# Retention and two MoE layers on one core: where moving and stationary operands begin within 64 bytes

## The chip, the cores and the metric

The kernel runs on one core of a Trainium2 chip. The metric is the device time of an execution, in microseconds, and the median over runs.

## The reference

Three layers follow each other. Batch 4, 8 heads, 768 positions, head size 64 give 3072 tokens of 512 features.

```python
# retention: per head a state S (64x64)
state = gamma * state + outer(k[t], v[t])
y[t]  = scale * q[t] @ state
# layer 1 (d_ff 2048)
h = x @ w_in
x = (h * sigmoid(1.702 * h)) @ w_out
# layer 2 (d_ff 1536)
gate = sigmoid(x @ w_gate)
out  = (gate * (x @ w_val)) @ w_out
```

Inputs are float32, the weights arrive as 64-bit words and are brought to float32 on the chip.

## The kernel before

**Products with three matmuls.** Nearly every product of 128x128 with 128x512 is done three times in float32r: each operand is split into a high part (a cast on ACT) and a low part (the original less the high part, on DVE or POOL), and high times high, high times low and low times high are summed in PSUM. In a matmul one operand is *stationary* (the weights that are loaded into the array, 128 columns) and one is *moving* (512 columns stream past it).

**Phase 1** goes through six blocks of 512 tokens. The attention of a block is worked out in items that are dealt out between the matmuls of the block before. For each block and each of 16 slices of d_ff there is a *unit*: `proj` (lines 268 to 273) multiplies the slice's weights `wh`, `wl` (stationary) with the block's tokens `xh`, `xl` (moving), twelve matmuls; `gated` and `gated_lo` make `gh`, `gl`; two units later `emit_out` (lines 357 to 382) multiplies the output weights `wh`, `wl` (stationary) with `gh`, `gl` (moving), twelve matmuls into four accumulators. The first eight units do this second product in plain float32, on unsplit tiles (line 373). `split_w` (lines 260 to 265) makes `wh` and `wl` in a pool of four. The tokens `xh`, `xl` lie in one of two pools, `xe` for even blocks and `xo` for odd ones (lines 59 and 299). The first two blocks are done half a d_ff at a time.

**Phase 2** has three groups of 1024 tokens and in each three rounds over a third of d_ff. A round has four *chains* (gate and value of two pairs of slices). A chain is seven products of 256-column halves that are combined so that eight are not needed: `product` (lines 526 to 536) multiplies chain weights `oh`, `ol` (stationary, made in `split_chain`, lines 515 to 524) with token halves and differences `xoh`, `xol` (moving), 42 matmuls in all. Chains alternate between two pools for their weights, `we` for even chains and `wo` for odd ones (`p2["w"][n % 2]`). `consume` (lines 543 to 563) makes the gated values `g2h`, `g2l`. At the end of a round `out_products` (lines 649 to 656) multiplies them with the output weights: here `g2h`, `g2l` are stationary and `woh`, `wol` move, 96 matmuls in a round.

**What sets the order.** It is written out by hand (`tc.manual_schedule`): each engine does its instructions in the order of the code. Pools are stacked from the left end and from the right end of a partition's memory (`left`, `right`, lines 49 to 65); a tile's place follows from the sizes of those before it.

**Where tiles begin.** The right-hand pools grow down from byte 229,344 of a partition, which is 32 past a multiple of 64, and nearly all tiles are multiples of 64 bytes long. So all that lies there up to the small constant tiles, and again behind them, begins 32 bytes past a multiple of 64; the left-hand pools begin at a multiple. The line that makes a weight pair in the kernel before:

```python
wh = wsp_p.tile([P, 512], F32R, name="wh", tag="wh")
```

Of the kernel before, what the change touches and what calls it, by code (L numbers as in the profile page):

```python
# [8 lines left out]
F32 = mybir.dt.float32  # L9
F32R = mybir.dt.float32r  # L10
# [5 lines left out]
P = 128  # L16
# [8 lines left out]
def retention_moe_moe2(  # L25
# [23 lines left out]
    left, right = (ctx.enter_context(ExitStack()) for _ in range(2))  # L49

    def pool(stack, name, bufs, side, **kw):
        return stack.enter_context(tc.tile_pool(name=name, bufs=bufs, side=side, reuse_waits="tile", **kw))

    PSUM = dict(space=bass.MemoryType.PSUM)
    dram = ctx.enter_context(tc.tile_pool(name="dram", bufs=1, space=bass.MemoryType.DRAM))
    wraw_p = pool(left, "wraw", NW, "left")
    wsp_p = pool(left, "wsp", 4, "left")
    g_p = pool(left, "g", 2, "left")
    x_p = [pool(right, "xe", 1, "right"), pool(left, "xo", 1, "left")]
    const = pool(right, "const", 1, "right")  # L60
# [15 lines left out]
    dv_sb = const.tile([P, CPB - 1, H], F32, name="dv_sb")  # L76
    dc_sb = const.tile([P, H], F32, name="dc_sb")
    dg_sb = const.tile([P, KC], F32, name="dg_sb")
    dm_sb = const.tile([P, 2, KC, C], F32, name="dm_sb")
    R = [const.tile([P, KC, P], F32, name=f"R{i}") for i in range(2)]  # L80

# [118 lines left out]
    def stage(n=1):  # L200

        for _ in range(min(n, len(to_stage))):
            ph, f, k = to_stage.popleft()
            t = cv_p.tile([P, 512], U64, name="w64", tag="w64", bufs=4)
            nc.sync.dma_start(out=t, in_=(w1 if ph == "1" else w2)[f, k])
            staged.append((ph, f, k, t))

    def convert(n, lo_engine):
# [48 lines left out]

        return scale, upper, lower, total

    def split_w(raw, lo_engine):  # L260
        wh = wsp_p.tile([P, 512], F32R, name="wh", tag="wh")
        wl = wsp_p.tile([P, 512], F32R, name="wl", tag="wl")
        nc.scalar.copy(wh, raw)  # L263
        lo_engine.tensor_tensor(out=wl, in0=raw, in1=wh, op=ALU.subtract)  # L264
        return wh, wl
# [74 lines left out]
    def split_out(i):  # L340

        j = i - DEPTH
        if WHOLE <= j < len(units):
            w_t[j, "out"] = split_w(raw1[units[j][1], 1], nc.gpsimd)

    def split_for(i):

        if i < len(units):
            b, f = units[i]
            w_t[i, 0] = split_w(raw1[f, 0], nc.gpsimd if i < 3 * FH else nc.vector)  # L350
# [65 lines left out]
    p2 = {}  # L416
# [14 lines left out]
    def tmp(name, bufs):  # L431
        return p2["tmp"].tile([P, 512], F32, name=name, tag=name, bufs=bufs)
# [82 lines left out]
    def split_chain(n, late):  # L515


        t, pl = wraw8[n], p2["w"][n % 2]
        a, b, engine = (S3, S4 + 1, nc.gpsimd) if late else (S1, A12 + 1, nc.vector)
        h, l = (pl.tile([P, b - a, 256], F32R, name=f"{x}{late:d}", tag=f"{x}{late:d}") for x in ("oh", "ol"))  # L520
        nc.scalar.copy(h, t[:, a:b])  # L521
        for j in range(a, b):
            wo[n, j] = (h[:, j - a], l[:, j - a])
        return lambda: engine.tensor_tensor(out=l, in0=t[:, a:b], in1=h, op=ALU.subtract)  # L524
# [13 lines left out]
    cb, gt, sgt, woh = {}, {}, {}, {}  # L538
# [4 lines left out]
    def consume(n, which, c):  # L543

        g, r, p, m = chains[n]
        if m == 0:
            yield
            sgt[p, which] = sg = tmp("sg", 4)
            nc.scalar.activation(out=sg, in_=c, func=AF.Sigmoid)
            yield  # L550
            yield
            return
        f, half = 2 * p + which // 2, which % 2
        if which == 0:
            for j in range(2):
                gt[f + j] = [p2["g2"].tile([P, 2, 512], F32R, name=x, tag=x) for x in ("g2h", "g2l")]
        gh, gl = (t[:, half, :] for t in gt[f])
        nc.vector.tensor_tensor(out=c, in0=c, in1=sgt.pop((p, which)), op=ALU.mult)
        yield
        nc.scalar.copy(gh, c)  # L560
        yield
        nc.vector.tensor_tensor(out=gl, in0=c, in1=gh, op=ALU.subtract)
        yield
# [12 lines left out]
    def middle(n):  # L576

        a, m1 = cb[n]
        b, d = bank2("pb"), bank2("pd")
        ahead = n + 1 < len(chains)  # L580
        if ahead and (n + 1) not in early:
            early[n + 1] = split_chain(n + 1, False)
        product(n, b, A12, B21, True, True)
        add(b, b, m1)
        while carried:
            next(carried.pop())
        c11 = consume(n, 0, b)
        next(c11)
        product(n, a, S2, T2, False, True)
        u2 = tmp("u2", 1)  # L590
        nc.scalar.copy(u2, a)
        if whole:
            whole.pop()
            split_out2()
        next(c11)
        if ahead:
            early.pop(n + 1)()
        product(n, d, S1, T1, True, True)
        product(n, a, S3, T3, False, True)
        u3, c22 = tmp("u3", 1), tmp("c22", 1)  # L600
        nc.scalar.copy(u3, a)
        next(c11)
        add(c22, d, u3)
        cb[n] = [a, d, u2, c22]

    def finish(n, last):
        a, d, u2, c22 = cb.pop(n)
        x22, x21, x12 = (consume(n, j, c) for j, c in ((3, c22), (2, a), (1, d)))
        next(x22)
        product(n, a, A22, T4, False, True)  # L610
        next(x22)
        next(x21)
        if not last:
            next(x22)
        product(n, d, S4, B22, False, True)
        next(x21)
        if last:
            next(x21)
        add(d, d, u2)
        next(x12)  # L620
        next(x22 if last else x21)
        if not last and n + 2 < len(chains):
            early[n + 2] = split_chain(n + 2, False)
        next(x12)
        if last:
            next(x12)
        else:
            carried.append(x12)
# [48 lines left out]
    with tc.manual_schedule():  # L677
# [9 lines left out]
        for t in range(1, 4):  # L687
            for i in (Q, K, V, KN):
                load_in(t, i, wraw_p, "wraw")
            stage()  # L690
        sig = const.tile([P, 1], F32, name="sig")
        nc.vector.memset(sig, 0.0)
        nc.scalar.activation(out=sig, in_=sig, func=AF.Sigmoid)
        warm = cv_p.tile([P, 512], F32, name="warm", tag="cva", bufs=3)
# [39 lines left out]
        for i, (b, f) in enumerate(units):  # L734
# [21 lines left out]
            n = blocks1[b][1]  # L756
# [30 lines left out]
            if b == len(blocks1) - 1:  # L787
                if f == 9:
                    sums(0)
                elif f in (11, 13):  # L790
                    split_chain(0, f == 13)()
# [144 lines left out]
```

## Time and profile before

| | |
|---|---|
| median of 3 runs | 1207.12 us (1205.52 to 1207.32) |
| span of the profiled execution, first to last instruction | 1204.5 us |
| the rest of a run's time, median less span | 2.6 us |
| PE busy | 1183.9 us (98%), 5916 matmuls |
| weight loads (PEld) | 948.8 us (79%) |
| DVE, ACT, POOL busy | 794.6, 541.4, 532.5 us |
| DMA queue q1 | 121.54 MB, 31.1% of 16 engines' span |
| HBM read, written | 98.31 MB, 24.12 MB |

The profiled execution's own time is listed as its span. Matmuls are pipelined, so a matmul's listed duration is longer than the distance to the start of the next; the ends are modelled, the starts are recorded. The plain float32 matmuls are recorded as two passes each, which is why PE has 5916 and not 5250. In the chain of waits a piece of PE is as long as the distance from one start (or end) to the next.

### The profile page before, as it was taken

How to read it: one execution, taken by the hardware profiler on the slowest of the kernel's cores; microseconds unless marked ns; L12 is line 12 of the kernel's file. 1: busy time of each engine (PE TensorE's matmuls, PEld its weight loads, DVE VectorE, ACT ScalarE, POOL GpSimd, SP SyncE). 2: the span in 40 equal slices, each digit the busy share in tenths (PEclk: the TensorE clock that was granted, in tenths of full speed). 3: DMA queues.
4: the chain of work that ended last, by engine and by line, in shares of the span. 5: the costliest groups of instructions: out<-in, count | busy, mean ns of one | idle time of the engine just before them, and what ended most of it. 6: DMA issues, size and time to landing. Idle time of an engine off the chain costs nothing.

```text
span 1204.5 us, 16042 instructions
## 1 busy us (share of the span) xinstructions
PE 1183.9 (98%) x5916; PEld 948.8 (79%) x5916; DVE 794.6 (66%) x1050; ACT 541.4 (45%) x948; POOL 532.5 (44%) x398
## 2 busy tenths in 40 slices
PE   7899999999999999999999999999999999999998
PEld 6656878877788887788788888888888888888887
DVE  6989999687588677766664636368535458535454
ACT  5424444444444444444554626164626164626151
POOL 5557874222322332322454626257625257635340
PEclk9999999999999999999999999999999999999999
DMA  8644245534335333412202202043212133212111
GB/s 324 208 160 140 88 158 167 192 115 140 123 100 163 123 114 133 131 52 79 70 1 88 80 27 79 27 135 110 72 34 71 36 115 115 86 35 70 37 36 70
DMA packets 62575, 123.48 MB, mean 103 GB/s; under 512 B 6816, under 2 KB 16288, under 8 KB 62496
## 3 DMA queue, kind: packets, MB, share of 16 engines
q1 hardware_dynamic: 61920, 121.54, 31.1%
q8 instruction: 46, 0.75, 0.3%
q10 hardware_dynamic: 576, 0.92, 0.2%
q14 instruction: 33, 0.27, 0.1%
HBM read 98.31 MB, written 24.12 MB: 102 GB/s over the span
## 4 chain that ended last, share of the span: by engine, by line
PE 87%; DVE 7%; issue 2%; DMA 2%; POOL 2%; ACT 1%; ACTq 0%; SPq 0%; DVEq 0%; POOLq 0%
PE pa L532 17%; PE pd L532 8%; PE acc L377 6%; PE h L273 6%; PE h L272 6%; PE h L271 6%; PE acc L378 6%; PE acc L379 6%; PE pb L532 4%; PE po L655 4%; PE po L656 4%; PE po L654 4%; DVE cva L234 2%; PE h L142 2%; DVE cva L231 2%
## 5 line engine op out<-in xcount | busy, mean ns | idle before, releaser
L264 POOL TENSOR_TENSOR wl<-wraw,wh 128x512 fp32r<-128x512 f32 x112 | 163.4, 1465 | 298.1 <-ACT wh L263 297.6
L273 PE MATMUL h<-xh,wl 128*128 128x512 f32 x384 | 152.0, 396 | 3.1 <-POOL wl L264 2.9
L271 PE MATMUL h<-xh,wh 128*128 128x512 f32 x384 | 154.2, 402 | 0.8 <-ACT xh L187 0.7
L272 PE MATMUL h<-xl,wh 128*128 128x512 f32 x384 | 150.9, 393 | 0.2 <-DVE xl L188 0.2
L377 PE MATMUL acc<-gh,wh 128*128 128x512 f32 x352 | 142.2, 404 | 1.4 <-DVE half L396 1.4
L378 PE MATMUL acc<-gh,wl 128*128 128x512 f32 x352 | 137.9, 392 | 0.0
L379 PE MATMUL acc<-gl,wh 128*128 128x512 f32 x352 | 137.2, 390 | 0.0
L263 ACT CAST wh<-wraw 128x512 fp32r<-128x512 f32 x184 | 109.1, 617 | 35.4 <-PE acc L379 34.6
L524 POOL TENSOR_TENSOR ol<-raw,oh 128x768 fp32r<-128x768 f32 x36 | 67.0, 1862 | 127.2 <-ACT oh L521 127.2
L281 ACT ACTIVATE sg<-h 128x512 f32<-128x512 f32 x88 | 52.6, 598 | 146.4 <-PE h L273 146.3
L282 DVE TENSOR_TENSOR sg<-h,sg 128x512 f32<-128x512 f32 x88 | 60.6, 688 | 86.3 <-ACT sg L281 85.9
L532 PE MATMUL pa<-xol,oh 128*128 128x512 f32 x288 | 114.0, 396 | 0.0
L532 PE MATMUL pa<-xoh,oh 128*128 128x512 f32 x288 | 113.3, 393 | 0.0
L532 PE MATMUL pa<-xoh,ol 128*128 128x512 f32 x288 | 112.8, 392 | 0.0
L287 ACT CAST gh<-sg 128x512 fp32r<-128x512 f32 x88 | 54.6, 621 | 98.2 <-DVE sg L282 98.2
L644 POOL TENSOR_TENSOR wol<-wor,woh 128x512 fp32r<-128x512 f32 x36 | 57.1, 1586 | 87.8 <-ACT woh L643 87.8
L273 PEld LDWEIGHTS h<-xh,wl 128*128 128x128 f32 x384 | 72.1, 188 | 23.5 <-POOL wl L264 6.9
L271 PEld LDWEIGHTS h<-xh,wh 128*128 128x128 f32 x384 | 72.2, 188 | 18.7 <-issue 1.7
L272 PEld LDWEIGHTS h<-xl,wh 128*128 128x128 f32 x384 | 72.1, 188 | 18.0 <-issue 1.9
L234 DVE SCALAR_TENSOR_TENSOR cva<-w,cva 128x512 uint32<-128x512 uint32 x68 | 84.4, 1241 | 2.3
L655 PE MATMUL po<-wol,g2h 128*128 128x512 f32 x216 | 84.4, 391 | 0.0
L656 PE MATMUL po<-woh,g2l 128*128 128x512 f32 x216 | 84.2, 390 | 0.0
(132 smaller groups left out, 2598.5 us busy)
## 6 DMA issues: line engine op xcount, KB each, us to landing
w<-in_w_dram SPq DMA_DIRECT2D x68, 512.0 KB, 3.7
in_t<-in_qkv_dram SPq DMA_DIRECT2D x93, 256.0 KB, 3.6
raw<-w2d SPq DMA_DIRECT2D x72, 256.0 KB, 3.1
w2d<-cva SPq DMA_DIRECT2D x36, 256.0 KB, 2.2
wor<-w2d SPq DMA_DIRECT2D x36, 256.0 KB, 2.7
out_dram<-ost SPq DMA_DIRECT2D x23, 256.0 KB, 2.0
xt<-x2d SPq DMA_DIRECT2D x18, 256.0 KB, 4.3
x2d<-ost SPq DMA_DIRECT2D x14, 256.0 KB, 2.8
```

The source lines that it names most:

```text
L234: nc.vector.scalar_tensor_tensor(out=ai, in0=hi, scalar=0x80000000, in1=ai, op0=ALU.bitwise_and, op1=ALU.bitwise_or)
L263: nc.scalar.copy(wh, raw)
L264: lo_engine.tensor_tensor(out=wl, in0=raw, in1=wh, op=ALU.subtract)
L271: nc.tensor.matmul(bank[:, :n], wh[:, k, :], xh[:, k, :n], start=(k == 0), stop=False)
L272: nc.tensor.matmul(bank[:, :n], wh[:, k, :], xl[:, k, :n], start=False, stop=False)
L273: nc.tensor.matmul(bank[:, :n], wl[:, k, :], xh[:, k, :n], start=False, stop=(k == KC - 1))
L377: nc.tensor.matmul(a, wh[:, wc], gh[:, :n], start=st, stop=False)
L378: nc.tensor.matmul(a, wl[:, wc], gh[:, :n], start=False, stop=False)
L379: nc.tensor.matmul(a, wh[:, wc], gl[:, :n], start=False, stop=sp)
L532: nc.tensor.matmul(bank, w[:, kk], x[:, k, :], start=start and k == 0 and w is wh and x is xh, stop=stop and k == 1 and w is wl, skip_grou ...
L655: nc.tensor.matmul(bank, gh, wl, start=False, stop=False)
L656: nc.tensor.matmul(bank, gl, wh, start=False, stop=f == FR - 1)
```

## The change

Tiles are moved within 64 bytes. A tile of 32 bytes, `edge`, is put at the right end ahead of all others, and the small tile `sig` is made among the constants instead of behind them; with both, all right-hand tiles that matmuls stream from begin at a multiple of 64 bytes. A function `shifted` makes a tile 16 elements (64 bytes) longer than needed and uses it from a given element on; the stationary operands of the three-matmul products are made with it.

| operand of the products | before: bytes past a multiple of 64 | after |
|---|---|---|
| `xh`, `xl` of even blocks (moving) | 32 | 0 |
| `xh`, `xl` of odd blocks (moving) | 0 | 0 |
| `wh`, `wl` of phase 1, both products (stationary) | 0 | 16 |
| `gh`, `gl` (moving) | 0 | 0 |
| `xoh`, `xol` (moving) | 32 | 0 |
| `oh`, `ol` of even chains (stationary) | 32 | 48 |
| `oh`, `ol` of odd chains (stationary) | 0 | 8 |
| `g2h`, `g2l` (stationary) | 0 | 40 |
| `woh`, `wol` (moving) | 0 | 0 |

The operands of attention's float32 matmuls go from 32 (some from 0) to 0.

```diff
+    pool(ctx, "edge", 1, "right").tile([P, 8], F32, name="edge")
...
+    sig = const.tile([P, 1], F32, name="sig")
...
+    def shifted(pool_, name, shape, floats, **kw):
+        n = 1
+        for d in shape[1:]:
+            n *= d
+        t = pool_.tile([shape[0], n + 16], F32R, name=name, tag=name, **kw)[:, floats:floats + n]
+        return t if len(shape) == 2 else t.rearrange("p (a b) -> p a b", a=shape[1])
+
     def split_w(raw, lo_engine):
-        wh = wsp_p.tile([P, 512], F32R, name="wh", tag="wh")
-        wl = wsp_p.tile([P, 512], F32R, name="wl", tag="wl")
+        wh = shifted(wsp_p, "wh", (P, 512), 4)
+        wl = shifted(wsp_p, "wl", (P, 512), 4)
...
-        h, l = (pl.tile([P, b - a, 256], F32R, name=f"{x}{late:d}", tag=f"{x}{late:d}") for x in ("oh", "ol"))
+        h, l = (shifted(pl, f"{x}{late:d}", (P, b - a, 256), 2 if n % 2 else 12) for x in ("oh", "ol"))
...
-                gt[f + j] = [p2["g2"].tile([P, 2, 512], F32R, name=x, tag=x) for x in ("g2h", "g2l")]
+                gt[f + j] = [shifted(p2["g2"], x, (P, 2, 512), 10) for x in ("g2h", "g2l")]
...
-        sig = const.tile([P, 1], F32, name="sig")
```

## Rows read from the trace of the kernel before

**Rows 1.** The page, parts 1 and 2: busy time, share and count; granted clock in tenths.

```profile
PE 1183.9 (98%) x5916; PEld 948.8 (79%) x5916; DVE 794.6 (66%) x1050; ACT 541.4 (45%) x948; POOL 532.5 (44%) x398
...
PEclk9999999999999999999999999999999999999999
```

**Rows 2.** Busy time by stretch: PE, PEld, DVE, ACT, POOL (counts), granted clock, DMA, GB/s.

```profile
0.00:60.00 60.00, 49.01 (x432) 36.91 (x433) 47.78 (x71) 28.65 (x62) 32.38 (x29) 1.00 0.76 266
60.00:120.00 60.00, 56.17 (x242) 36.88 (x241) 53.82 (x68) 22.17 (x40) 37.97 (x27) 0.97 0.47 152
120.00:180.00 60.00, 58.44 (x251) 46.45 (x250) 59.32 (x64) 28.73 (x54) 47.65 (x31) 1.00 0.38 123
180.00:300.00 120.00, 120.00 (x746) 96.79 (x745) 92.33 (x135) 54.77 (x100) 40.78 (x30) 1.00 0.47 152
...
780.61:841.30 60.69, 60.69 (x265) 49.51 (x264) 43.61 (x52) 32.06 (x55) 38.62 (x27) 1.00 0.34 111
```

**Rows 3.** Groups by form on PE and PEld: count, busy us, mean ns, idle before.

```profile
L271 PE MATMUL h<-xh,wh 128*128 128x512 f32 x384 | 154.2, 402 | 0.8 <-ACT xh L187 0.7
...
L377 PE MATMUL acc<-gh,wh 128*128 128x512 f32 x352 | 142.2, 404 | 1.4 <-DVE half L396 1.4
...
L271 PEld LDWEIGHTS h<-xh,wh 128*128 128x128 f32 x384 | 72.2, 188 | 18.7 <-issue 1.7 <-ACT xh L187 0.9 <-ACT wh L263 0.5
```

**Rows 4.** PE's timeline in an odd block (block 3): start us, us, instruction.

```profile
415.39 0.40 PE L378 MATMUL acc<-gh,wl 128*128 128x512 f32 x1
...
417.90 0.39 PE L271 MATMUL h<-xh,wh 128*128 128x512 f32 x1
...
420.39 0.39 PE L273 MATMUL h<-xh,wl 128*128 128x512 f32 x1
```

**Rows 5.** The same in an even block (block 4).

```profile
467.26 0.40 PE L271 MATMUL h<-xh,wh 128*128 128x512 f32 x1
...
468.20 0.40 PE L272 MATMUL h<-xl,wh 128*128 128x512 f32 x1
468.44 0.40 PE L273 MATMUL h<-xh,wl 128*128 128x512 f32 x1
...
469.84 0.40 PE L273 MATMUL h<-xh,wl 128*128 128x512 f32 x1
```

**Rows 6.** Chain of waits, pieces of an odd chain, then an even one: start, us.

```profile
734.01 1.40 PE pd L532 x6
...
736.79 1.37 PE pa L532 x6
738.16 1.36 PE pd L532 x6
```

**Rows 7.** PE's timeline, output products of a round: the first and the sixty-first start.

```profile
761.55 0.39 PE L654 MATMUL pd<-woh,g2h 128*128 128x512 f32 x1
...
775.15 0.40 PE L532 MATMUL pa<-xoh,oh 128*128 128x512 f32 x1
```

**Rows 8.** Chain of waits: eight passes of plain float32 in phase 1.

```profile
98.76 3.43 PE acc L373 x8
```

**Rows 9.** ACT's timeline, casts for successive chains; the page's group of POOL's subtractions.

```profile
725.16 1.05 ACT L521 CAST oh<-raw 128x1024 fp32r<-128x1024 f32 x1
...
735.26 1.05 ACT L521 CAST oh<-raw 128x1024 fp32r<-128x1024 f32 x1
...
L264 POOL TENSOR_TENSOR wl<-wraw,wh 128x512 fp32r<-128x512 f32 x112 | 163.4, 1465 | 298.1 <-ACT wh L263 297.6
```

**Rows 10.** PE's timeline in an even chain: two neighbouring starts.

```profile
651.60 0.39 PE L532 MATMUL pa<-xoh,oh 128*128 128x512 f32 x1
651.82 0.39 PE L532 MATMUL pa<-xol,oh 128*128 128x512 f32 x1
```

## The prediction, made before the changed kernel ran

> **What bounds the kernel now.** I read the page's first two parts first. [...] Then the busy time by stretch: after the first 180 us PE is busy for all of each stretch, and before that it is idle for 11.0, 3.8 and 1.6 us of three times 60 [rows 2]. So from 180 us on nothing is late for PE, and the time is the number of matmuls times the distance between two starts. A PE that is always "busy" can still be slow, so I read the distance from the starts in the timeline and from the pieces of the chain of waits, not from the durations: a matmul of 512 columns is listed with 0.39 us, but the next starts after 0.23.
>
> Nearly all work is one form, a float32r matmul of 128x512 whose weights are loaded while the one before streams (188 ns of weight load, one for each matmul) [rows 3]. By the loops there are 4584: 576 projections of even blocks, 576 of odd blocks, 1056 of phase 1's second product, and in phase 2 nine rounds of 168 chain and 96 output matmuls, 2376. Their start-to-start distance differs with nothing but the place of the operands:
>
> - moving and stationary operand both at a multiple of 64 bytes: an odd block's twelve projections stand 226 ns apart (2.49 us in 11 steps), and the output products of phase 2 stand 13.60 us / 60 = 226.7 ns apart [rows 4, 7]. Behind an interruption by attention some steps are longer: over the second product and the projection together it is 5.00 / 22 = 227.3 [rows 4].
> - both 32 bytes off (even chains): 2.73 / 12 = 227.5 ns [rows 6].
> - moving 32 off, weights at a multiple: an even block's projections stand 2.58 / 11 = 234.5 ns apart, with a single step of 0.24 among them [rows 5]; an odd chain takes 1.40 / 6 = 233.3 [rows 6].
>
> A round of phase 2, one part of each kind, is 60.69 us for 264 matmuls, 229.9 each [rows 2]. [...]
>
> **What the change does, part by part.** No instruction is added, removed or moved on any engine. One wait for a DMA, once in the kernel, where phase 2 opens, stands one instruction earlier on ACT, on a copy into `u2` or `u3` and not on the sigmoid behind it. I cost it at nothing: it is the same load, and ACT has time to wait, idle for over half of each stretch [rows 2]; at the most it is one such instruction's place in a queue that PE does not wait for in that stretch.
>
> *Moving operands to multiples of 64.* This touches the even blocks' projections (234.5 ns) and all chains. Alone, with weights that fit, the step would be the locked one, 226.7: it saves 576 x 7.8 = 4.5 us in phase 1 and 2376 x 3.2 = 7.6 in phase 2; the other 1632 of phase 1 lose their rest, 0.6 each, 1.0. Together 13.1 us.
>
> *Weights off by 16, 48, 8 and 40.* No row has such a place. All steps of the kernel, also the 1632 + 864 that are now at 226.7, get a new one, so this is the larger term and the unknown one. [...] What is known is that displacing the weights by half of 64 bytes moves the step by 233.3 - 226.7 = 6.6 ns, and that single steps of about 0.22 occur between longer ones [rows 10]. [...] I take half of the known effect, as a gain: 226.7 - 3.3 = 223.4 ns, near those short steps. Then phase 2 saves 2376 x (229.9 - 223.4) = 15.4 us, the 1632 save 1632 x 3.9 = 6.4, the even blocks 576 x 11.1 = 6.4, in all 28.2. This includes the 13.1 above.
>
> What of it lies on the path: from 180 us on all of it. In the first 180 us PE waits 16.4 us for others [rows 2], so a shorter step becomes a longer wait; I take off a tenth of the phase 1 part, 1 us. Does something else then come late? DVE is busy 92 of 120 us in the fullest stretch behind 180 us, and POOL 41 of 120 [rows 2]; 3% less time leaves both below 80%.
>
> *Writes into displaced tiles.* ACT and DVE or POOL write the halves. A cast into a chain's tile takes 1.05 us whether it lands 32 off or at a multiple [rows 9], so I cost it at nothing. Offsets of 8 and 16 have no row. A worse price is covered: POOL waits 297.6 us for ACT in the weight splits [rows 9]; were each of its subtractions (1465 ns, 112 of them) half as long again, 82 us, that wait would shrink first. Without that cover each microsecond would count, in the first 180 us above all. From below, a cheaper write gains nothing, as PE does not wait for it there.
>
> The sum is made on the profiled execution: span 1204.5 - 27.2 = 1177.3. The median of the three runs, 1207.12, is 2.6 us over that span, for what lies around it, so 1180 us.
>
> [...] The rows show the step of one and the same moving stream at 227.5 or 233.3 ns with weights in two places [rows 6]. [...]
>
> **The rivals.**
>
> 1. *Only the moving side counts; weights off are neither good nor bad.* Every step is 226.7: 13.1 us, with 1 us for the start 12, so 1195. For: 226.7 is what all well-placed rows settle on, sixty in a row [rows 7]. Against: weights do matter in the chains [rows 6].
> [...]
> 3. *Slower: what is good is that both operands stand alike.* The two fast kinds in the rows, 0 with 0 and 32 with 32, are alike, and the slow one is not [rows 4, 6]; after the change nothing is alike. The place is every stream of both phases, the price 233.3 a step: phase 2 loses 2376 x 3.4 = 8.1 us, the 1632 of phase 1 lose 9.8, the even blocks gain 0.7: +17.2, so 1224. It decides as soon as the mean step is over 229.6, what the 4584 have now (weighting 229.9, 227.3 and 234.5). For: it is the plainest reading of the four kinds of rows. Against: "alike" may only stand for one good displacement among several. At 240 for all it would be +48, 1255.
> [...]
>
> **How the numbers follow.** My forecast (1180, its own range 1172 to 1188) 0.32; rival 1 (1195) 0.20; rival 2 (1165) 0.20; rival 3 (1224, between 1210 and 1235) 0.19; rival 4 0.09. A measurement of this kernel can tell 0.2%, 2.4 us, from no change. Faster: 0.32 + 0.20 + 0.20 = 0.72; same, of rival 4 and the edge of 1 and 3, 0.08; slower 0.20. The range takes in rivals 1 and 2 but for the part below 1160 (0.06), and goes up to 1214, so that most of rival 3 (0.13) is left out: 0.19 in all.
>
> **What would show it.** In the timeline behind the change: twelve projections of an even block as far apart as those of an odd one; the odd and even chains' pieces of six at 1.34 us, a round at 59.0 us; the sixty output steps of 13.60 us at 13.40. PE still at 98% and the listed durations of a matmul a little below 0.39. I am wrong if the sixty output steps rise above 13.60 (rival 3: 14.0), if they stay there (rival 1), or if PE waits grow behind 180 us. If steps at 0 and off by 8 differ from those off by 16 by more than 5 ns, the offset within 16 bytes is what counts, which none of the cases has.

## The result, and the profile after

The changed kernel takes 1217.82 us in the median of 4 runs (1217.28 to 1218.37), the kernel before 1206.44 beside it: a ratio of 1.0096, 95% interval 1.0081 to 1.011. It is slower by 1%, where 2% faster was forecast, and lies above the stated range (1160 to 1214). The profiled execution has a span of 1216.5 us, 12.0 more than before.

The page's busy times and clock of the changed kernel, beside [rows 1]:

```profile
PE 1197.0 (98%) x5916; PEld 952.7 (78%) x5916; DVE 784.7 (65%) x1050; ACT 541.3 (44%) x948; POOL 530.6 (44%) x398
...
PEclk9989999999999999999999999999999999999999
```

PE is still the bound, with 13.1 us more work in the same 5916 instructions; DVE, ACT and POOL were busy no longer than before. The 8 in the clock's third slice is a short fall, 0.94 in the mean of 60 to 120 us where [rows 2] have 0.97. The stretches, beside [rows 2], the second one a round of phase 2:

```profile
180.00:300.00 120.00, 120.00 (x744) 96.46 (x742) 90.90 (x134) 54.64 (x99) 42.00 (x31) 1.00 0.47 150
...
726.88:788.24 61.36, 61.36 (x265) 49.67 (x264) 30.51 (x40) 24.41 (x40) 24.50 (x20) 1.00 0.17 52
```

No wait came in behind 180 us. The round takes 61.36 us where it took 60.69: 232.4 ns a matmul and not 229.9. The timeline at the places of [rows 4, 5, 7] shows where (start, us; odd block, even block, output products):

```profile
419.01 0.39 PE L387 MATMUL acc<-gh,wl 128*128 128x512 f32 x1
...
421.56 0.39 PE L280 MATMUL h<-xh,wh 128*128 128x512 f32 x1
...
424.12 0.40 PE L282 MATMUL h<-xh,wl 128*128 128x512 f32 x1
...
471.64 0.40 PE L280 MATMUL h<-xh,wh 128*128 128x512 f32 x1
...
474.19 0.39 PE L282 MATMUL h<-xh,wl 128*128 128x512 f32 x1
...
768.72 0.40 PE L663 MATMUL pd<-woh,g2h 128*128 128x512 f32 x1
...
782.71 0.39 PE L541 MATMUL pa<-xoh,oh 128*128 128x512 f32 x1
```

The odd block's twelve went from 226 to 2.56 / 11 = 233 ns, the second product with it to 5.11 / 22 = 232; the even block's fell from 234.5 to 2.55 / 11 = 232; the sixty output steps rose from 13.60 to 13.99 us, 233.2 each. In the chain of waits, beside [rows 6], an odd chain's piece and two of an even one:

```profile
740.98 1.41 PE pd L541 x6
...
743.78 1.39 PE pa L541 x6
745.16 1.39 PE pd L541 x6
```

The odd chain stays slow, the even one lost what it had. So all stages now stand near 232. The mean distance between two starts, over all float32r matmuls that the next one follows within 250 ns, is worked out from the recorded starts, here and for the runs below:

| mean step, ns | projections, even blocks | odd blocks | second product | even chains | odd chains | outputs |
|---|---|---|---|---|---|---|
| before | 234.1 | 226.8 | 228.6 | 229.5 | 233.6 | 227.5 |
| changed | 232.1 | 231.9 | 232.3 | 231.0 | 233.4 | 232.9 |
| number | 530 | 557 | 1010 | 756 | 756 | 863 |

The differences times the numbers are 11.2 us, nearly all of the 12.0.

### The profile page after: what moved, and what is told of

It reads as the page before. It is cut to its first block, busy times and chain, and to the rows that moved or that the text cites. A ratio compares the mean times of both kernels' runs of the same rounds, so it can differ in the third digit from the quotient of the medians.

```text
span 1216.5 us, 16042 instructions
## 1 busy us (share of the span) xinstructions
PE 1197.0 (98%) x5916; PEld 952.7 (78%) x5916; DVE 784.7 (65%) x1050; ACT 541.3 (44%) x948; POOL 530.6 (44%) x398
## 4 chain that ended last, share of the span: by engine, by line
PE 87%; POOL 5%; DVE 4%; issue 2%; DMA 1%; ACT 0%; ACTq 0%; SPq 0%; DVEq 0%; POOLq 0%
PE pa L541 17%; PE pd L541 8%; PE acc L386 6%; PE h L282 6%; PE h L280 6%; PE h L281 6%; PE acc L387 6%; PE acc L388 6%; PE po L664 4%; PE po L665 4%; PE pb L541 4%; PE po L663 4%; POOL wl L273 3%; PE h L144 2%; POOL wraw L256 2%
## 5 line engine op out<-in xcount | busy, mean ns | idle before, releaser
L273 POOL TENSOR_TENSOR wl<-wraw,wh 128x512 fp32r<-128x512 f32 x112 | 166.6, 1494 | 297.5 <-ACT wh L272 297.0
L533 POOL TENSOR_TENSOR ol<-raw,oh 128x768 fp32r<-128x768 f32 x36 | 61.4, 1706 | 132.5 <-ACT oh L530 132.5
L663 PE MATMUL po<-woh,g2h 128*128 128x512 f32 x216 | 85.0, 394 | 0.0
```

Of the source, the lines that this page charges most:

```text
L663: nc.tensor.matmul(bank, gh, wh, start=f == 0, stop=False)
```

## The experiments

### What is alike?

The first theory was the prediction's third rival: stationary and moving operand should stand alike within 64 bytes. **e1_all_zero** keeps the change but uses every stationary tile from its beginning, `oh`, `ol`, `g2h` and `g2l` like `wh` and `wl`:

```diff
-        wh = shifted(wsp_p, "wh", (P, 512), 4)
-        wl = shifted(wsp_p, "wl", (P, 512), 4)
+        wh = shifted(wsp_p, "wh", (P, 512), 0)
+        wl = shifted(wsp_p, "wl", (P, 512), 0)
...
```

> The moving side stays at multiples of 64 bytes and all stationary operands go to multiples of 64 too. Theory A (what counts is how far the stationary operand stands from the moving one within 64 bytes, and 0 is best): all steps 226.5 to 228.5 ns, a round of phase 2 at 59.9 us, 1192 to 1197 us. Theory B (the moving operand's place alone counts): as the changed kernel, 1218 us. Theory C (each operand counts for itself, best at a multiple of 64): as A here.

Measured: 1213.83 us, ratio to the kernel before 1.0054 (1.004 to 1.0067). Theories A and C missed by 17 us, B by 4. Everything begins at a multiple of 64, and yet the sixty output steps, which were at 226.7 ns with both operands at such multiples, take 13.89 us, 231.5 each:

```profile
766.71 0.40 PE L663 MATMUL pd<-woh,g2h 128*128 128x512 f32 x1
...
780.60 0.39 PE L541 MATMUL pa<-xoh,oh 128*128 128x512 f32 x1
```

The other stages are at 230.5 to 231.8. What this kernel still has from the change is `edge` and the 64 bytes by which `shifted` makes every tile longer.

**e2_no_edge** leaves the `edge` line out of the changed kernel and keeps all else.

> The displaced stationary operands stay, the tile at the right end goes, so that even blocks and all chains stream from 32 bytes off again, and even chains have their weights at 16 (48 from the moving side, as in the changed kernel), odd chains at 8 (40 from it), even blocks 16 (48 from it). Theory A: even chains keep the changed kernel's 231.0 ns, odd chains come near its output products' 232.9, odd blocks stay; 1214 to 1220 us. Theory C: both operands of the chains are off, so all chains are slower than with one off, 235 ns or more, 1222 us or more. Theory B: even blocks and chains 5 to 7 ns slower than in the changed kernel, 1227 us.

Measured: 1215.52 us, ratio 1.0068 (1.0054 to 1.0081), so `edge` gains nothing here. Even chains 231.3, odd chains 232.1, even blocks 231.5, odd blocks 232.4: moving them back to 32 past a multiple of 64 changed no stage by over 1.3 ns. Theories B and C, which wanted slower chains, fall; theory A's time and steps hold within 1 ns in this run.

**e3_alike_off** puts the chains' moving tiles into longer tiles too and both operands 16 off, displaces phase 1's low part alone by 32, and gives the output products their old tiles back:

```diff
-        wh = shifted(wsp_p, "wh", (P, 512), 4)
-        wl = shifted(wsp_p, "wl", (P, 512), 4)
+        wh = shifted(wsp_p, "wh", (P, 512), 0)
+        wl = shifted(wsp_p, "wl", (P, 512), 8)
...
-            [p2["x"].tile([P, 2, 512], F32R, name=f"{n}{j}", tag=f"{n}{j}") for n in ("xoh", "xol")] for j in range(7)
+            [shifted(p2["x"], f"{n}{j}", (P, 2, 512), 4) for n in ("xoh", "xol")] for j in range(7)
...
-        h, l = (shifted(pl, f"{x}{late:d}", (P, b - a, 256), 2 if n % 2 else 12) for x in ("oh", "ol"))
+        h, l = (shifted(pl, f"{x}{late:d}", (P, b - a, 256), 4) for x in ("oh", "ol"))
...
-                gt[f + j] = [shifted(p2["g2"], x, (P, 2, 512), 10) for x in ("g2h", "g2l")]
+                gt[f + j] = [p2["g2"].tile([P, 2, 512], F32R, name=x, tag=x) for x in ("g2h", "g2l")]
```

> Chains: moving and stationary both 16 off. Output products: both at 0. Phase 1: moving at 0, the high part of the weights at 0, the low part at 32. Theory A: chains 226.5 to 228.5 ns. Theory C: chains 231 ns or more. Phase 1 tells whose weight load counts: if that of the next matmul, loaded while one streams, the step of a matmul with xl or gh on wh that is followed by wl (L281 of the projections, L386 of the second product) is the slow one; if its own, the matmul with wl (L282, L387).

Measured once: 1212.38 us. Chains at 230.6 and 232.4 though alike, so theory A falls; the outputs in their old tiles are back at 227.7. Phase 1 tells nothing: with longer tiles the distances are mixed anyway.

**e4_curve_1** has the changed kernel's tiles with other displacements (8 floats in phase 1; 6 and 14 in even and odd chains; 2 in the outputs).

> Moving at 0 everywhere; stationary at 32 in phase 1, 24 in even chains, 56 in odd chains, 8 in the output products. Theory A: 32 gives 233 to 235 ns as in the kernel before's even blocks and odd chains, 8 gives 233.4 as in the changed kernel's odd chains whatever the stage; 24 and 56 between 229 and 235, none below 226.7. A theory by which some displacement is better than none: one of 24 and 56 below 226.

Measured once: 1221.81 us. The stages' mean steps are 231.3 to 234.9 ns, none below 226.7; of the output products 54 take a step of 260 ns each, which the mean of 234.9 counts in. This run could not tell displacements apart: like the three before, it mixes each with the 64 bytes by which the tiles grew.

### The distance modulo 256, at each step

In the kernel before, the tiles of the products are 2048, 3072, 4096 or 8192 bytes long, all multiples of 1024, so all tiles of one kind begin at the same place modulo 256. With 64 bytes more each, the tiles of a pool go through 0, 64, 128 and 192 modulo 256. Sorted by the distance of stationary from moving operand modulo 256, the kernel before has 0 in all its fast stages and 160 in both slow ones. **e5_one_distance** is the kernel before with one line, which brings right-hand and left-hand tiles to the same place modulo 256:

```diff
+    pool(ctx, "edge", 1, "right").tile([P, 24], F32, name="edge")
```

> The kernel before with 96 bytes at the right end, no tile longer than it was: all moving and stationary operands of the float32r products begin at 128 past a multiple of 256. Theory A is dropped, as all at multiples of 64 still took 231 ns. Theory D (what counts is the distance of stationary from moving modulo 256, and that it is 0 at each step; tiles made 64 bytes longer break that): all steps 226.5 to 228, 1192 to 1197 us. Rival E (the longer tiles are not to blame, but that right-hand tiles moved): steps near 231, 1211 to 1215 us.

Measured: 1196.42 us, ratio 0.9916 (0.9902 to 0.993), faster than both kernels and as theory D forecast; rival E, which wanted steps near 231, falls. Its page, a round, an even block's twelve, the sixty output steps:

```profile
PE 1172.6 (98%) x5916; PEld 948.2 (80%) x5916; DVE 797.5 (67%) x1050; ACT 541.3 (45%) x948; POOL 533.3 (45%) x398
```

```profile
714.40:774.30 59.90, 59.90 (x265) 49.43 (x264) 31.28 (x40) 24.41 (x40) 25.15 (x20) 1.00 0.17 53
```

```profile
464.31 0.39 PE L272 MATMUL h<-xh,wh 128*128 128x512 f32 x1
...
466.80 0.39 PE L274 MATMUL h<-xh,wl 128*128 128x512 f32 x1
...
755.27 0.39 PE L655 MATMUL pd<-woh,g2h 128*128 128x512 f32 x1
...
768.87 0.39 PE L533 MATMUL pa<-xoh,oh 128*128 128x512 f32 x1
```

The even block's steps fell from 234.5 to 2.49 / 11 = 226.4 ns [rows 5], a round from 60.69 to 59.90 us [rows 2]. In this kernel distances of 0, 256, 512 and 768 modulo 1024 all occur, as right-hand and left-hand tiles differ by 256, and all are fast, with stage means at most 1.2 ns above 226.7: 256 counts as 0.

**e6_longer_tiles** adds to it the 64 bytes, without displacement, in phase 1 and, likewise, in `g2h` and `g2l`; `shifted` makes a tile 16 elements longer here and uses its first part:

```diff
-        wh = wsp_p.tile([P, 512], F32R, name="wh", tag="wh")
-        wl = wsp_p.tile([P, 512], F32R, name="wl", tag="wl")
+        wh = shifted(wsp_p, "wh", (P, 512))
+        wl = shifted(wsp_p, "wl", (P, 512))
...
```

> As the one before, but the weights of phase 1 and the stationary operand of the output products in tiles 64 bytes longer, used from their beginning: they stand 0, 64, 128 or 192 from the moving side modulo 256, in turn. Theory D: phase 1 and output products 231 to 232.5 ns, chains stay at 226.5 to 228; 1206 to 1211 us. Rival E: no step differs from the run with 96 bytes at the right end.

Measured: ratio 0.9993 (0.9984 to 1.0002), at the lower edge of theory D's times. The stages with longer tiles go up to 230.8 to 231.5, the outputs to 231.0; the chains, whose tiles were left alone, keep 226.9 to 227.4. A chain's piece and the sixty output steps:

```profile
737.18 1.36 PE pd L540 x6
```

```profile
764.47 0.40 PE L662 MATMUL pd<-woh,g2h 128*128 128x512 f32 x1
...
778.36 0.39 PE L540 MATMUL pa<-xoh,oh 128*128 128x512 f32 x1
```

The chain's piece is 226.7 ns a matmul; the outputs take 13.89 us for sixty, as in the run with everything at 0. So the longer tiles alone, with no operand displaced and no tile on the moving side lengthened, do the harm. Only the weights' place was changed here, and the step went from 226.7 to 231.5 ns. By what way the place acts on the step, no run shows.

**e7_constant_1** and **e8_constant_2** keep tiles of the old length and shift whole pools, so that the distance is constant in each stage but not 0 (the first is shown; the second has 48, 56 and 32 elements):

```diff
+    pool(ctx, "edge", 1, "right").tile([P, 16], F32, name="edge")
...
+    pool(left, "gap", 1, "left").tile([P, 16], F32, name="gap")
     g_p = pool(left, "g", 2, "left")
...
+            if name == "wout":
+                pool(ctx, "gap3", 1, "left").tile([P, 48], F32, name="gap3")
```

> Tiles of the old length, so distances are the same at each step, but not 0: 192 in odd blocks and the second product, 224 in even blocks and odd chains, 64 in the output products; even chains stay at 0. Theory D, strict (0 alone is good): 231 to 235 ns in these stages. Theory D, loose (any distance, so long as it stays): 226.5 to 228.

> The same with 32 in odd blocks and the second product, 96 in even blocks and odd chains, 128 in the output products. Theory D, strict: 231 to 235 ns; loose: 226.5 to 228, which the 160 of the kernel before (233.3 in odd chains) speaks against.

Measured once each: 1210.51 and 1216.5 us. An odd block's twelve at 192 (e7), the last sixty output steps of a round at 64 (e7) and at 128 (e8):

```profile
389.95 0.39 PE L273 MATMUL h<-xh,wh 128*128 128x512 f32 x1
...
392.47 0.39 PE L275 MATMUL h<-xh,wl 128*128 128x512 f32 x1
```

```profile
823.61 0.40 PE L658 MATMUL pd<-woh,g2h 128*128 128x512 f32 x1
...
837.61 0.39 PE L536 MATMUL pa<-xoh,oh 128*128 128x512 f32 x1
```

```profile
829.82 0.39 PE L658 MATMUL pd<-woh,g2h 128*128 128x512 f32 x1
...
843.82 0.39 PE L536 MATMUL pa<-xoh,oh 128*128 128x512 f32 x1
```

That is 2.52 / 11 = 229 ns and twice 14.00 / 60 = 233.3. Mean steps by constant distance, modulo 256: 32 gives 233.3, 64 gives 233.2, 96 gives 233.8 to 233.9, 128 gives 233.1, 224 gives 233.0 to 233.1, and 192 only 229.0 to 229.5; with the 160 of the kernel before, 233.6 to 234.1. 128 is slow (233.1) where 256 was fast (at most 227.9 in e5), so half the length is not enough. Even chains, at 0 in both, stay at 228.6 and 227.3; both their operands begin 160 (e7) and 32 (e8) past a multiple of 256, where in e5 both begin at 128. So it is the distance that counts, not the place itself. The loose form of theory D falls; the strict one held, but for 192.

### The change's parts apart

**e9_edge_alone** is the kernel before with the change's first part, `edge` of 32 bytes and `sig` among the constants.

> The change's first part alone: 32 bytes at the right end and the small tile among the constants, so that right-hand tiles begin at multiples of 64; no longer tiles, no displaced weights. Theory D: modulo 256 the distance in even blocks and odd chains goes from 160 to 192, which as a constant distance took 229.0 to 229.5 ns in the run with 192; so 4 to 5 ns less in 576 projections and 756 chain matmuls, the rest as before or a little better: 1199 to 1203 us. Theory B (the moving side at a multiple of 64 is what gains): these stages at 226.7, 1195 us.

Measured: 1201.55 us, ratio 0.9957 (0.9944 to 0.9969). An even block's twelve and an odd chain's piece:

```profile
466.94 0.40 PE L273 MATMUL h<-xh,wh 128*128 128x512 f32 x1
...
469.48 0.40 PE L275 MATMUL h<-xh,wl 128*128 128x512 f32 x1
```

```profile
732.22 1.37 PE pd L534 x6
```

2.54 / 11 = 231 and 1.37 / 6 = 228 ns, 230.4 and 229.2 in the mean: better than 234 and 233, as the distance is 192 now and not 160, but not the 226.7 that multiples of 64 would give if they were the point.

With this run the change comes apart into steps that each differ in one thing, in the ratio to the kernel before: `edge` and `sig`, 0.9957; the longer tiles on top, 1.0054; the displacements on top, 1.0096. Of 1207 us that is 5 gained, then 12 and 5 lost.

**e10_displaced_constant** asks for the displacements alone. On the fast kernel, high and low part go into one tile that is 256 bytes longer, at the change's 16 in phase 1 and 40 in the outputs:

```diff
+    def pair(pool_, name, n, floats):
+        t = pool_.tile([P, 2 * n + 64], F32R, name=name, tag=name)
+        return t[:, floats:floats + n], t[:, floats + n:floats + 2 * n]
...
+        wh, wl = pair(wsp_p, "wh", 512, 4)
...
+                gt[f + j] = [x.rearrange("p (a b) -> p a b", a=2) for x in pair(p2["g2"], "g2h", 1024, 10)]
```

> As the run with 96 bytes at the right end, with the change's displacements of 16 in phase 1 and 40 in the output products, but high and low part of a stationary operand in one tile 256 bytes longer, so that the distance is the same at each step. Theory D, strict: the displacement alone is slow too, 230 to 235 ns in these stages, chains 226.7 to 228, 1208 to 1216 us. Rival F (only the changing distance is slow, small displacements within 64 bytes are harmless): as the run with 96 bytes, 1196 us.

Measured: 1202.05 us, ratio 0.9961 (0.9948 to 0.9974), between the two theories, and both miss. The sixty output steps at 40, and two stretches of phase 1 at 16, of which the rows of L275, each third matmul, are shown:

```profile
764.30 0.39 PE L658 MATMUL pd<-woh,g2h 128*128 128x512 f32 x1
...
777.90 0.39 PE L536 MATMUL pa<-xoh,oh 128*128 128x512 f32 x1
```

```profile
414.24 0.39 PE L275 MATMUL h<-xh,wh 128*128 128x512 f32 x1
...
414.92 0.39 PE L275 MATMUL h<-xh,wh 128*128 128x512 f32 x1
...
415.60 0.39 PE L275 MATMUL h<-xh,wh 128*128 128x512 f32 x1
...
421.00 0.40 PE L275 MATMUL h<-xh,wh 128*128 128x512 f32 x1
...
421.70 0.40 PE L275 MATMUL h<-xh,wh 128*128 128x512 f32 x1
...
422.40 0.40 PE L275 MATMUL h<-xh,wh 128*128 128x512 f32 x1
```

At 40 the outputs take 13.60 us, 226.7 each, as at 0. At 16 the same three matmuls, at the same distance, take 0.68 us in one unit and 0.70 in the next: 226.7 or 233.3. At 16 a stream settles on one of two steps, and either can come out. Matmuls of attention part the two units shown. This trace has 54 streams of phase 1 with nine or more steps that nothing interrupts: 18 go at 226.7 and 36 at 233.3, and none changes after its first three steps; the longest have 149 and 320 steps.

**e11_low_part_apart** gives phase 1's low parts a pool of their own, 96 from the moving side, on the fast kernel.

> As the run with 96 bytes at the right end, but phase 1's low parts in a pool of their own, 96 from the moving side; high parts at 0. If the load of the next weights is what collides with the stream, the slow step is that of the matmul ahead of the one with the low part (L276 in the projections, L381 in the second product), by 5 ns or more over the others' mean; if its own weights count, the matmul with the low part is (L277, L382). If all three are alike, near 231, the phase that a step leaves to the next decides and not the single load.

Measured once: 1203.78 us. The third outcome. Four starts in a row, three steps of 0.23 to 0.24:

```profile
420.10 0.40 PE L275 MATMUL h<-xh,wh 128*128 128x512 f32 x1
420.34 0.40 PE L276 MATMUL h<-xl,wh 128*128 128x512 f32 x1
420.57 0.39 PE L277 MATMUL h<-xh,wl 128*128 128x512 f32 x1
420.80 0.40 PE L275 MATMUL h<-xh,wh 128*128 128x512 f32 x1
```

The means in the projections are 232.5 on L275, 231.7 on L276 and 231.9 on L277. One stationary operand of three at another distance makes all three steps slow, also the one with high parts at 0 before and behind it. So a mixture of distances can be nearly as bad as a bad one.

What a change of distance costs stands in the trace of the kernel before. There the matmuls of an even chain, at 0, follow those of an odd one, at 160; the first, the tenth and the twenty-second start:

```profile
735.24 0.40 PE L532 MATMUL pb<-xoh,oh 128*128 128x512 f32 x1
...
737.32 0.39 PE L532 MATMUL pa<-xoh,oh 128*128 128x512 f32 x1
...
740.04 0.39 PE L532 MATMUL pa<-xoh,oh 128*128 128x512 f32 x1
```

Nine steps take 2.08 us, 231 ns each, and the next twelve 2.72 us, 226.7. The outputs of a round settle likewise: the start at 761.55 in [rows 7] is the thirty-seventh of 96 and not the first, and the mean of all is 227.5. In the changed kernel the distance changes after twelve matmuls at the latest, and no twelve steps in a row of one stage have a mean under 229.7 ns; of its 96 unbroken twelves of projections (11 steps), though, ten go at 226.6 to 227.2. That a stream there mostly has no time to settle fits these numbers; no run tried it by itself.

**e12_displaced_constant_2** tries the rest of the change's displacements in the same way: 48 and 8 in even and odd chains, and 40 in phase 1.

> As the run with constant displacements before, but 40 in phase 1, and the change's 48 in even and 8 in odd chains; output products at 0. Theory G (a constant distance is needed, and only some distances settle; 0 and 40 do, 16, 64, 96, 128, 160, 192 and 224 don't): phase 1 settles at 40 as the output products did, 226.7 to 228.5 ns; for 48 and 8 no run has a constant distance: between 226.7 and 234. If the stage and not the distance decided at 40: phase 1 above 230 ns. Time 1197 to 1207 us.

Measured: 1210.1 us, ratio 1.0033 (1.002 to 1.0046), above the forecast times. An odd block's twelve (the low part lies in the same tile, so its row carries that name):

```profile
417.35 0.40 PE L275 MATMUL h<-xh,wh 128*128 128x512 f32 x1
...
419.92 0.39 PE L277 MATMUL h<-xh,wh 128*128 128x512 f32 x1
```

2.57 / 11 = 233.6 ns: phase 1 at 40 settles on the slow step, where the outputs at 40 settled on the fast one. Theory G falls as it was put: at 40 the distance modulo 256 alone does not decide. 48 gives 233.4, 8 gives 230.9.

## Why the prediction was wrong, point by point

*What bounds the kernel* held: PE back to back, the time being the number of matmuls times their step, and nothing else late. The float32r step does depend on where operands stand, but not, as the text has it, on "nothing but" that: at distance 0 it is also longer for the first nine steps or so behind a slow neighbour, 231 ns in the even chain from 735.24 us on.

*"Moving operands to multiples of 64 ... the step would be the locked one, 226.7"* failed by its unit. I read the two slow stages as 32 bytes off within 64; they are 160 off within 256. With `edge` alone they are 192 off, and the step is 229 to 230 and not 226.7: 5 us and not the 13.1 of the term. Of the others the rows could not tell 64 from 256: only 0 and 160 occur in them.

*"Weights off by 16, 48, 8 and 40 ... I take half of the known effect, as a gain"* put a loss down as a gain. No stage's row spoke for a gain, and no run shows a stage at the 223.4 ns of the term: the four kinds of rows in the text all said that what is equal is fast. The step of 0.22 in [rows 10] is one of six, from 650.89 to 652.29, that take 1.40 us, 233.3 each. The term adds 15 us of gain to the 13.1; the displacements cost some 5 us on top of the longer tiles. No stage's mean came to the 240 ns that the text names with its third rival: the highest is 234.9, with single steps of 260 (e4).

*"No instruction is added, removed or moved"* was true, and hid the largest term. I took from the layout where the first tile of a kind begins, and not that tiles of 64 bytes more do not all begin alike. That alone costs 12 us and turns the sign: with `edge` and the longer tiles, but no displacement, the ratio is already 1.0054. It stood in the diff: `n + 16`.

*The third rival* had the side and nearly the size: "nothing is alike", 233.3 a step, 1224 us, against a mean of 232.3 and 1217.8. Its reason was half of it: alike means the same distance modulo 256 at each step. It had 0.19 where the rows gave it the plainest case. *The first rival* (1195) is ruled out by the changed kernel, whose moving operands all begin at multiples of 64, and by the run with everything at 0, 1213.8. *The second* (1165, steps of 220 ns) has no run near it: no stage of any run settled below 226.7.

*Writes into displaced tiles* cost nothing that shows: ACT was busy 541.3 us after, 541.4 before.

## What to carry to other kernels

Where streams of float32r matmuls run back to back, look at the distance between starts, not at PE's busy share (98% at 1196.42 us and at 1217.82 alike), and sort it by the place of the stationary operand against the moving one modulo 256 bytes. Give both the same place there, at every tile of the pool: here a pad that was put once, at the right end, did it (e5, 1196.42 us, output steps of 226.7 ns), and a pad of 64 bytes in every tile undid it (e6, 231.5 ns). A mean step that is the same in all stages after a change that touched them differently points to something that all of them share.

## What the runs showed of the hardware

In these runs, what a float32r stream settles on depends on the distance of stationary from moving operand modulo 256 bytes, so long as it is constant: 226.7 ns at 0, 229 at 192, and means of 233 to 234 at 32, 48, 64, 96, 128, 160 and 224. At 8 the mean is 230.9, and no step was settled on. 226.7 and 233.3 are 6.7 ns apart; at 16 either came out, and at 40 the lower one in the outputs and the higher one in phase 1.

At 0 a stream came back to 226.7 behind an interruption or a neighbour at another distance. In the kernel before this took eight or nine steps in the even chains and the outputs, and four or five in 28 of the 37 streams of phase 1 that settled. With 0 in all stages (e5) these steps raise a stage's mean by 1.2 ns at most; in the kernel before they raise that of the even chains, which stand between odd ones, to 229.5.

What makes the step longer, and why one stationary operand in three slows its neighbours too, was not found: the run made for it (e11, 232.5, 231.7 and 231.9 ns) only showed that it is not a single load's matter. That the state in which a stretch begins decides between two steps fits all this, the 54 streams at 16 above all, but was not tried by itself. The passes of plain float32 show no such cost: their starts stand 429 ns apart in the median of every run [rows 8], at distances of 0, of 192 (e7) and of 32 (e8).
